# Moving a weight conversion between the slots of a fused top-k attention and GELU MLP

## The chip, the core and the metric

The kernel runs on one core of a Trainium2 chip. The core has a matrix engine (TensorE, PE in the profile), a vector engine (VectorE, DVE), a scalar engine (ScalarE, ACT), GpSimd (POOL) and an engine that here only issues DMAs (SyncE, SP). Each works through its own instruction queue in order and waits at semaphores for the others. The metric is the device time of one execution in microseconds; lower is better. Four runs of the kernel before took 1640.07 to 1641.21 us, median 1640.57.

## The reference

Attention with a top-k mask, then an MLP with an exact GELU:

```python
scores = scale * q @ k.T                        # (8, 8, 576, 576), head_dim 64
kth    = 32nd largest of each row of scores
scores = where(scores >= kth, scores, -1e9)
attn   = exp(scores - max); attn /= sum + 1e-9
x      = (attn @ v) -> (4608, 512)              # heads side by side
h      = x @ w_in                               # (512, 2048)
out    = gelu_exact(h) @ w_out                  # (2048, 512)
```

q, k and v are float32. Both weight matrices arrive as 64-bit floats, and the kernel makes float32 of them on the chip, with integer operations on their halves.

## The kernel before

**Items and slots.** Attention is cut into 144 items. An item is one block of 128 query rows for two heads (or the 64-row tails of two pairs), so two score rows of 576 per partition. The main loop runs over slots n = 0 to 147. Slot n holds the steps of four items at once, a pipeline by hand: scores of item n+2 (PE, copied out by ACT), the top-k of item n (DVE: eight MAX8 and six MATCH_REPLACE8, then the reciprocal `rden` of item n-1), the softmax of item n-1 (ACT: for each of its two rows e a Prelu that drops what is below the threshold, and an Exp that also sums into `den`), the transposes of item n-2 (PE into PSUM, copied to `pt` by ACT: the tails, then main 0, main 1), and the product with v of item n-3 (PE tile `o`, in even slots only, since two items share one; a copy to `xT` by ACT follows).

**What links the engines.** POOL makes the threshold of item n when its top-k is done (`neg`, `bias`, L355 and L358), adds the small constant to `den` (L372) when ACT has both sums, and multiplies the exponentials with `rden` (`normalise`, L392, two instructions); the transposes need these products. In some slots `normalise` runs on DVE instead. DVE's `rden` waits for POOL's L372, which waits for ACT's second softmax. The order on every engine is the order of the calls in the loop; nothing reorders them.

**PSUM.** The tag `tp` has two buffers, handed out in turn to the score tails `t_ps`, the product `o`, the transposes and the q/k transposes (`tp_qk`). So `o` holds one buffer until ACT has copied it to `xT`, and the second transposes after it (main 0) need that buffer.

**The MLP.** The loop calls `mlp` between the steps, which issues matmul pieces as soon as all heads of a block of tokens have their `xT`. The first block is complete in slot START = 10. In slots 10 and 11 at most four pieces are issued, later eight. What is left when the attention is done is issued behind the loop.

**The weights.** They are converted in 16 units of two blocks of 128 x 512. `ORDER` lists the units, `SLOT_OF` gives each its slot. For the unit of slot n: two DMAs of 512 KB bring its 64-bit words (`load_weights`, issued by SP at the end of slot n-2), ACT makes integer parts of them at the end of slot n-1 (`weights_size`, L175, L177 and, if POOL does not do it, L179), and in slot n POOL adds two parts (`weights_add`, L194) and the third (`weights_end`, L206). Where `on_pool` holds, POOL also does the multiplication (L191) in ACT's stead and `normalise` of that moment runs on DVE; where `ends_late` holds, the second addition stands in the middle of the slot, behind L372. The words lie in the upper half of `w_out_sb`, in one of two regions by the parity of the unit's place in `ORDER`; three units have a tile `words` of their own, because the region is by then in use. A region is loaded again when `weights_end` of its last unit is done.

Below are the functions that the diff touches and what calls them, with the line numbers of the profile.

## Time and profile before

| | us |
|---|---|
| median of four runs (lowest, highest) | 1640.57 (1640.07, 1641.21) |
| the profiled execution: time, span | 1640.07, 1638.3 |
| PE, DVE, ACT, POOL busy | 1586.6, 1415.0, 1185.2, 662.3 |
| a unit on ACT: L175, L177, L179, each | 1.24, 1.24, 1.13 |
| a unit on POOL: L194, L206, each; L191 where it runs | 2.40, 2.40; 3.12 |
| `normalise` of one item: POOL, DVE | 3.4, 0.95 |
| softmax of one row: L379, L380 and its accumulator read | 0.78, 0.78, 0.19 |
| DVE from slot to slot, slots 1 to 10 | 9.70 |

The span is what lies between the first and the last instruction; the time is 1.8 us longer. The first MAX8 of a slot marks where the slot begins on DVE: 10.68 us for slot 0, 20.34, 30.04, 39.74, 49.44, 59.15, 68.85, 78.55, 88.25, 97.95 for slots 1 to 9, 107.66 for slot 10, and 117.36, 129.13, 140.96, 151.73, 163.60, 173.32, 186.19, 195.91 and 206.35 for slots 11 to 19. The other engines begin their part of a slot earlier or later; ACT's parts of slots 4 to 9 begin some 3.5 us after DVE's. In the rows of a timeline the columns are the start, the time from the first start to the last end of the merged instructions, engine, line, operation, tiles, count, and in square brackets the idle time of the engine just before, with what ended it.

### The profile page before, as it was taken

To read this page: it belongs to the slowest core of one execution; us is meant where nothing else is said; L and a number is where in the kernel's file an instruction comes from. 1 tells how busy PE (TensorE), PEld (TensorE's weight loads), DVE (VectorE), ACT (ScalarE), POOL (GpSimd) and SP (SyncE) were. 2 spreads that over 40 slices of the span, in tenths; PEclk is the share of its full clock that TensorE was granted. 3 is DMA by queue.
4 is the path that set the end of the run, shared out by engine and by line. 5 is a ranking of instruction groups with operands and counts; after the bars stand their busy time and mean duration, and the time that the engine had idled before them with its cause. 6 is when DMAs were issued, how large, how long until landed. Compare 5 with 4: busy or idle time off the path is not lost.

```text
span 1638.3 us, 25030 instructions
## 1 busy us (share of the span) xinstructions
PE 1586.6 (97%) x8818; PEld 1075.4 (66%) x8818; DVE 1415.0 (86%) x3046; ACT 1185.2 (72%) x2133; POOL 662.3 (40%) x759
## 2 busy tenths in 40 slices
PE   6579999999999999999999999999999999999999
PEld 4356676766666666676666667676666666666665
DVE  7999999988898899998989898998889889999800
ACT  6999877777777777777777777777777777777720
POOL 4897533333333333333333333333333333333300
PEclk7779999999999999999999999999999999999999
DMA  6433110011101120001110111001110101000000
GB/s 166 142 110 121 55 43 1 14 33 40 35 1 28 30 50 8 14 16 36 30 28 15 28 30 43 1 14 32 41 36 1 28 16 35 1 14 3 5 13 13
DMA packets 126765, 56.14 MB, mean 34 GB/s; under 512 B 117776, under 2 KB 118064, under 8 KB 126640
## 3 DMA queue, kind: packets, MB, share of 16 engines
q1 hardware_dynamic: 125376, 54.12, 12.3%
q8 instruction: 70, 1.15, 0.3%
q10 hardware_dynamic: 1200, 0.39, 0.1%
q14 instruction: 55, 0.45, 0.1%
q0 software_dynamic: 64, 0.03, 0.0%
HBM read 45.08 MB, written 9.44 MB: 33 GB/s over the span
## 4 chain that ended last, share of the span: by engine, by line
PE 92%; ACT 5%; POOL 1%; issue 1%; DVE 1%; DMA 1%; SPq 0%; ACTq 0%; POOLq 0%; DVEq 0%
PE y_ps L554 30%; PE h_ps L518 30%; PE o L466 9%; PE tp L429 8%; PE s_ps L287 8%; PE tp_qk L242 2%; PE t_ps L283 2%; PE o L477 1%; ACT s L380 1%; PE s_ps L314 1%; PE tp_t L411 1%; ACT s L379 1%; POOL s L392 1%; ACT w_in_sb L175 1%; ACT s L297 1%
## 5 line engine op out<-in xcount | busy, mean ns | idle before, releaser
L340 DVE MAX8 top<-rest 128x8 f32<-128x576 f32 x864 | 608.8, 745 | 0.0
L518 PE MATMUL h_ps<-xT,w_in_sb 128*128 128x256 f32 (+1 forms) x2560 | 553.1, 361 | 0.0
L554 PE MATMUL y_ps<-w_out_sb,g 128*128 128x512 f32 x1152 | 548.9, 599 | 0.0
L392 POOL TENSOR_SCALAR s<-s,rden 128x576 f32<-128x576 f32 x278 | 476.5, 1723 | 0.6 <-DVE rden L366 0.4
L518 PEld LDWEIGHTS h_ps<-xT,w_in_sb 128*128 128x128 f32 x2560 | 428.4, 191 | 61.8 <-issue 16.8
L343 DVE MATCH_REPLACE8 rest<-top,rest 128x576 f32<-128x576 f32 x576 | 422.9, 741 | 0.0
L372 POOL TENSOR_SCALAR den<-den 128x2 f32<-128x2 f32 x144 | 32.0, 222 | 836.7 <-ACT s L380 836.3
L554 PEld LDWEIGHTS y_ps<-w_out_sb,g 128*128 128x128 f32 x1152 | 195.2, 190 | 168.2 <-issue 167.3
L297 ACT ACTIVATE s<-s_ps 128x1024 f32<-128x1024 f32 x127 | 130.4, 1027 | 164.7 <-PE s_ps L287 143.0
L380 ACT ACTIVATE s<-s,bias 128x576 f32<-128x576 f32 x288 | 223.3, 775 | 13.2 <-ACT s L379 0.8
L379 ACT ACTIVATE s<-s,neg 128x576 f32<-128x576 f32 x288 | 224.1, 778 | 0.3 <-POOL neg L355 0.2
L436 ACT COPY pt<-tp 128x512 f32<-128x512 f32 x256 | 147.1, 575 | 101.8 <-PE tp L429 101.8
L429 PEld LDWEIGHTS tp<-ident,s 128*128 128x128 f32 x1152 | 145.6, 144 | 100.5 <-issue 58.9
L343 DVE MATCH_REPLACE8 rest<-top,s 128x576 f32<-128x576 f32 x288 | 211.5, 742 | 0.0
L340 DVE MAX8 top<-s 128x8 f32<-128x576 f32 x288 | 201.6, 741 | 1.4 <-ACT s L293 1.4
L429 PE MATMUL tp<-ident,s 128*128 128x128 f32 x1152 | 177.8, 278 | 13.9 <-ACT pt L412 11.5
L466 PE MATMUL o<-pt,raw_v 128*64 128x256 f32 x1280 | 156.3, 392 | 0.0
L287 PE MATMUL s_ps<-qk 64*128 64x256 f32 x1024 | 150.9, 415 | 0.8 <-ACT s L295 0.8
L366 DVE RECIPROCAL rden<-den 128x2 f32<-128x2 f32 x144 | 23.0, 159 | 137.6 <-POOL den L372 137.3
L466 PEld LDWEIGHTS o<-pt,raw_v 128*64 128x64 f32 x1280 | 88.2, 140 | 66.6 <-issue 24.0
L287 PEld LDWEIGHTS s_ps<-qk 64*128 64x128 f32 x1024 | 91.1, 192 | 23.4 <-issue 1.3
L529 ACT ACTIVATE g<-h_ps 128x512 f32<-128x512 f32 x144 | 78.6, 595 | 37.8 <-PE h_ps L518 37.1
(71 smaller groups left out, 1073.9 us busy)
## 6 DMA issues: line engine op xcount, KB each, us to landing
raw_q<-in_q_dram SPq DMA_DIRECT2D x64, 128.0 KB, 2.4
raw_v<-in_v_dram SPq DMA_DIRECT2D x64, 128.0 KB, 2.4
w_out_sb<-in_moe_w_in_dram SPq DMA_DIRECT2D x16, 511.8 KB, 4.9
raw_k<-in_k_dram SPq DMA_DIRECT2D x62, 128.0 KB, 2.4
out_dram<-y SPq DMA_DIRECT2D x31, 256.0 KB, 2.2
w_out_sb<-in_moe_w_out_dram SPq DMA_DIRECT2D x10, 511.8 KB, 3.8
words<-in_moe_w_out_dram SPq DMA_DIRECT2D x6, 511.8 KB, 4.5
out_dram<-y SPq DMA_DIRECT2D x9, 128.0 KB, 2.3
```

The lines of the kernel that those rows point to most:

```text
L287: nc.tensor.matmul(s_ps[:, e, c * 256 : (c + 1) * 256], lhsT=lhsT[rows, :], rhs=qk[rows, KT + c * 256 : KT + (c + 1) * 256], start=True, s ...
L297: nc.scalar.activation(spread(s, S + TL, SM), s_ps, func=AF.Copy, scale=scale)
L340: nc.vector.max(st["top"][:, e, 8 * r : 8 * r + 8], cur[e])
L343: nc.vector.match_replace(rest[:, e], st["top"][:, e, 8 * r : 8 * r + 8], cur[e], LOWEST)
L379: nc.scalar.activation(s, s, func=AF.Prelu, bias=st["neg"][:, e, 1:2], scale=1.0, alpha=STEEP)
L380: nc.scalar.activation(s, s, func=AF.Exp, bias=st["bias"][:, e : e + 1], scale=1.0, accum_out=st["den"][:, e : e + 1],)
L392: (nc.vector if e >= 2 - on_dve else nc.gpsimd).tensor_scalar(s, s, st["rden"][:, e : e + 1], None, op0=ALU.mult)
L429: nc.tensor.transpose(tp[:, j * P : (j + 1) * P], s[:, first + j * P : first + (j + 1) * P], ident)
L436: nc.scalar.copy(out=dst, in_=tp.rearrange("p (j n) -> p j n", j=NM))
L466: nc.tensor.matmul(o[e * D : (e + 1) * D, 0:n], lhsT=vt[:, j, e, :], rhs=pt[:, e * NM + j if j < NM else 2 * NM, :], start=(j == 0), stop= ...
L518: nc.tensor.matmul(h_tile(u)[:, i, :], lhsT=w_in_sb[:, ko, f * P : (f + 1) * P], rhs=xT[:, ko, c0 : c0 + n], start=(ko == 0), stop=(ko == ...
L554: nc.tensor.matmul(y_of[sub], lhsT=g_of[u][:, i, sub * P : (sub + 1) * P], rhs=w_out_sb[:, f, :], start=(f == 0), stop=(f == FT - 1),)
```

## The change

The units move. Before, unit i of the order had slot i + 1, the last one slot 17. After, units 0 to 9 have slots 0 to 9, and the last six have slots 11, 13, 14, 15, 16 and 18; slots 10, 12 and 17 have none. With the slots move the DMAs, ACT's operations one slot earlier and POOL's. The third unit's words go to a tile of their own. All of the last six now have their multiplication on POOL (five before), and `normalise` runs on DVE at the end of slots 10, 12, 13, 14, 15 and 17 (before: 11, 12, 13, 14 and 16). The second addition of the first unit stands in slot 1, beside that of the second.

Up to slot 9 both rows of the softmax now stand ahead of the copy to `xT`; before, the copy stood between them. Slot 10 keeps the order it had.

```diff
-    FIRST = 1
     START = 2 * NP + 2
...
-    SLOT_OF = {u: FIRST + i + (i == UNITS - 1) for i, u in enumerate(ORDER)}
+    SLOT_OF = dict(zip(ORDER, [*range(START), 11, 13, 14, 15, 16, 18]))
...
-        if i not in (12, 14, 15):
+        if i not in (2, 12, 14, 15):
             at = FT // 2 + 4 * (i % 2)
...
     def on_pool(u):
-        return u in words and SLOT_OF[u] >= START + 2
+        return u in words and SLOT_OF[u] > START
...
     def ends_late(u):
-        return u in words and SLOT_OF[u] <= START
+        return u in words and SLOT_OF[u] < START
...
     for n in range(2):
-        load_weights(FIRST + n)
+        load_weights(n)
...
+    weights_size(unit_in(0))
...
         if n <= START:
             softmax(n - 1, 0)
+        if n < START:
+            softmax(n - 1, 1)
         copy_x()
         mlp(1)
...
-        if not late:
+        if n == START:
             softmax(n - 1, 1)
...
-        if ends_late(unit_in(n)):
-            weights_end(unit_in(n))
+        for u in (unit_in(0), unit_in(1)) if n == 1 else (unit_in(n),) if n > 1 else ():
+            if ends_late(u):
+                weights_end(u)
...
-        if n >= FIRST:
-            load_weights(n + 2)
+        load_weights(n + 2)
```

## The prediction

> **What bounds the kernel now.** I read the page's slices first, then busy time slot by slot, then the chain of waits up to 250 us, then POOL's and PE's timelines. The slices:

> ```profile
> PE   6579999999999999999999999999999999999999
> DVE  7999999988898899998989898998889889999800
> PEclk7779999999999999999999999999999999999999
> ```

> A slice is 41 us. PE is full from the fourth on; nothing behind it touches a weight conversion. What can move is where PE's full stretch begins, and its gaps. The slots 9 to 12 (columns: length, then busy time and count of PE, PE weight loads, DVE, ACT, POOL; granted clock, DMA share, GB/s):

> ```profile
> 97.95:107.66 9.71, 4.17 (x21) 2.80 (x20) 9.71 (x24) 8.83 (x16) 8.86 (x8) 0.74 0.30 108
> 107.66:117.36 9.70, 9.56 (x50) 6.50 (x51) 9.70 (x24) 9.28 (x17) 8.20 (x8) 0.73 0.32 111
> 117.36:129.13 11.77, 9.75 (x60) 7.62 (x58) 10.74 (x25) 10.88 (x18) 11.27 (x11) 1.00 0.63 189
> 129.13:140.96 11.83, 11.06 (x67) 8.63 (x65) 10.77 (x24) 11.66 (x20) 8.87 (x7) 1.00 0.27 97
> ```

> Up to slot 10 DVE has no gap, and ACT and POOL are within a microsecond of it. From slot 10 on PE is full but for the difference of the first two figures: 0.14, 2.02 and 0.77 us. What starts slot 10's MLP stands in the chain (start, length, what):

> ```profile
> 96.37 0.67 PE tp L429 x4
> 97.06 0.52 ACT pt L436
> ...
> 98.04 1.26 ACT w_out_sb L175
> ...
> 106.01 1.13 PE tp L429 x4
> 107.17 0.59 ACT pt L436
> 107.80 0.80 PE t_ps L283 x2
> 108.60 2.01 PE s_ps L287 x8
> 110.61 3.46 PE o L466 x20
> 114.33 0.87 PE h_ps L518 x4
> ```

> From 64.8 to 107.8 us the chain is ACT and the transposes it waits for; then PE runs slot 10's scores and `o`, and the first MLP matmul follows. So ACT's pace through slots 1 to 9 sets where the long stretch begins, and DVE is close beside it. PE's later gaps:

> ```profile
> 125.24 0.66 PE L429 MATMUL tp<-ident,s 128*128 128x128 f32 x4 [0.64 <-ACT pt L412]
> 127.77 0.49 PE L283 MATMUL t_ps<-qk 128*128 128x128 f32 x2 [1.39 <-ACT pt L436]
> 137.47 0.66 PE L429 MATMUL tp<-ident,s 128*128 128x128 f32 x4 [0.77 <-ACT pt L412]
> 199.97 0.30 PE L416 MATMUL tp_t<-ident,s 128*64 128x128 f32 x1 [0.71 <-POOL s L392]
> ```

> They are 3.5 us together: the most that relief behind slot 10 can give. It is also 0.2% of the time, about what a measurement of this kernel can tell from no change.

> **The change part by part**, followed along ACT.

> *First unit, slot 0.* A unit's three ACT operations take 3.47 us (19.89 to the next scores copy at 23.36). They now follow the q/k copy at 14.78, in ACT's own idle time (1.65 and 1.20 us before rows there): 15.3 to 18.75, if the words have landed (issued from 7.79, landing after 3.6 to 6.8 us: yes). Scores copy (1.06) and q/k copy (0.48) follow, so unit 1 starts at 20.3, 0.4 us behind where unit 0 started. ACT is one unit further and 0.4 us late. SP issues the third unit's two DMAs (1.0 us) at 21.5 instead of 30.5 into a tile of its own; v's four issues behind them, 1 us later, are read only at 52.5.

> *POOL in slot 1: the first cost.* Before:

> ```profile
> 28.11 2.41 POOL L206 TENSOR_TENSOR w_in_sb<-w_in_sb,w_out_sb 128x1024 int32<-128x1024 int32 x1
> 30.48 0.23 POOL L355 TENSOR_SCALAR neg<-top 128x4 f32<-128x4 f32 x1
> 30.79 0.19 POOL L358 TENSOR_TENSOR bias<-neg 128x2 f32<-128x2 f32 x1
> 30.97 3.44 POOL L392 TENSOR_SCALAR s<-s,rden 128x576 f32<-128x576 f32 x2
> ```

> Now two additions stand behind L372: 28.4 to 33.2 (2 x 2.37). Queued behind them are `neg` and `bias` (33.7) and `normalise` (37.1 against 34.4). ACT's softmax of item 1 waits for `neg` (33.5 against 32.83) and ends at 36.8; the tails' transposes wait for `normalise`: 37.2 against 34.46. In slot 2 the q/k transposes and the tails' were ready before ACT came for them (36.05); now ACT waits for both, and the next unit starts at 41.2 instead of 39.14. ACT is 2.0 us late. POOL's L372 of slot 2, behind L194 (37.1 to 39.6), makes `rden` 0.2 us late on DVE.

> *Copy behind both softmaxes, slots 4, 6, 8.* In slot 4 ACT saves its 0.30 us wait for `o`. But main 0 needs the buffer that this copy frees. Before, PE made main 0 during the second softmax. Now ACT waits: copy 0.35, transposes 0.66, minus the tails' copy in between. From the copy's start to the next unit was 3.31 us in slot 6, with 1.58 of softmax in it: 1.73. Now: 1.10 to main 0's copy, then two copies, 2.08. Cost 0.35 each in slots 6 and 8, 0.05 in slot 4. Queued behind on ACT: main 1, the next unit, scores, softmax; behind those L372 and `rden`. The price rests on PE's full clock. The nearest rows on both sides: main 0 at 75.59 after 1.32 us of idle PE took 0.65; main 1 at 47.11 after 1.96 us took 1.12, with the granted clock at 0.50 in that slot. PE's gap ahead of main 0 grows from 1.3 to 2.9 us. At half clock both transposes cost 1.30 a slot instead of 0.35. I take 0.35, because a gap of 4.49 us (60.3 to 64.80) still started at full clock (0.33 for one transpose); the upper end stays in the range.

> [...] The trace shows drops after 3.55 and 3.66 us and none at the start after 4.49. [...]

> *To slot 9.* ACT's units before started at 39.14, 49.60, 59.44, 69.05, 78.50, 88.09, 98.04, 107.91. From 41.2 with the same steps and these costs: 51.7, 61.55, 71.15, 80.95, 90.55, 100.85, and slot 9's last copy 2.8 us later than before. ACT does not catch up: its steps are 9.5 to 10.4, DVE's 9.70. DVE now waits for L372 in slots 2, 4, 5 and 9, 1.3 us together, inside ACT's 2.8. Loads still land in time: they go out later with POOL, but are used later too.

> *Slots 9 to 12: the gain.* The unit that ACT did at 107.91 is gone, but the MLP's start waits for PE's `o`, not for ACT: nothing. So it starts at 114.2 + 2.8. At slot 10's end ACT does 2.45 us for the next unit instead of 3.47; the tails of slot 11 come 1.0 earlier, which removes the gap of 0.64; main 0 then waits for PE, and main 1's copy still stands behind the second softmax, so 0.47 of 2.02 us is gained. At slot 11's end no unit (2.45): the gap of 0.77 goes. DVE's `normalise` at slot 10's end (0.95) replaces slot 11's; POOL does slot 11's in 3.4 us, 3 us before PE needs it. POOL's 7.9 us of unit 10 end at 126 + 2.8, before L372's sums.

> *Slots 15 to 18.* The unit of slot 16 adds 2.45 us on ACT at 175.6, where ACT had 0.51 and 0.93 us idle: the tails' copy goes from 180.46 to 182.3, and main 0, which needs its buffer, 0.6 us late on PE. POOL's `normalise` at slot 16's end (3.4 us, DVE's 0.95 before) ends at 189.3 against PE's tails at 189.99: covered by 0.7, else the excess counts in full. At slot 17's end DVE's `normalise` removes the 0.71 us gap at 199.97. Slot 18's unit falls on 1.1 us of idle ACT, and its PE matmuls do not wait for it.

> Sum: +2.8 - 0.5 - 0.8 + 0.6 - 0.7 = +1.4. The profiled execution of 1640.07 (span 1638.3 and 1.8 around it) gives 1641.5; it stood 0.5 below the median, so against the median 1642.0.

> **The rivals.**
> A. *Clock stays up, ACT's delay is hidden.* PE's gaps in slots 5, 7 and 9 shorten, because ACT comes 2 to 3 us later and `normalise` only 1.6 to 2.5. If the clock holds there, each main 1 takes 0.66 instead of 1.12 (1.4 together), and slot 10's `t_ps`, `s_ps` and `o` take 0.49, 1.13 and 2.38 instead of 0.80, 2.08 and 3.53 (2.4 together). Then 1.4 - 3.8 = -2.4: 1638.2. [...]
> B. *Half clock in slots 4, 6 and 8.* Main 0 and main 1 of the product slots at 1.1: 3 x 0.95 more, +4.3: 1644.9. It decides (3.3 us) from two of the three slots on. For: main 1 at 47.11. Against: the 4.49 gap.
> C. *The move is hidden.* POOL's second addition is absorbed because ACT's wait in slot 2 only replaces waits for the half-clock transposes there (0.72 and 0.27 us idle) and the rest is regained behind slot 10: -0.5 to +0.5, about 1640.6. Against: ACT has no idle time in slots 3 to 9 to catch up.

> **How the numbers follow.** Forecast 0.42 (1640.9 to 1643.4 by itself), A 0.24, B 0.22, C 0.12. Faster by over 0.2% (below 1637.3): less than half of A, whose middle lies 0.9 above that bound, 0.10. Slower (above 1643.8): nearly all of B and 0.05 of the forecast, 0.25. The rest 0.65. The range reaches down into A to 1637.7, with 0.1 of it left out below, and up to 1645.8, which is B and 0.9 us of waits in slots 16 to 18.

> **What would show it.** Right: `neg` of slot 1 near 33.3 us and `normalise` near 33.7; a unit on ACT at about 41; ACT idle some 0.7 us ahead of main 0 in slots 4, 6 and 8; the first MLP matmul near 117; no wait at L412 in slots 11 and 12, a wait of some 1.5 us for main 1's copy at the end of slot 11. Wrong: the first MLP matmul at or before 114; words that land late in slot 0 or 2; the granted clock in slots 4 to 10 far from 0.7 to 0.8; waits of PE behind slot 13 that before did not have.

## The result and the profile after

The changed kernel took 1644.41 us (median of 35 runs, 1642.62 to 1647.14), the kernel before 1640.97 (55 runs, 1639.53 to 1643.60). The ratio is 1.0021 with a 95% interval of 1.0016 to 1.0026: 3.4 us slower (2.6 to 4.3), against a forecast of 1.4. The profiled execution took 1643.92 us with a span of 1642.1, 3.8 more than before. In it DVE starts slot 0 0.2 us later, because k's first load landed later (PE waited 0.21 us for it).

The page's slices after:

```profile
PE   5569999999999999999999999999999999999999
DVE  7999989988898989998989888998889888999800
PEclk7769999999999999999999999999999999999999
```

The picture is the same: PE and its clock differ in the first three slices of 41 us alone, where PE is a little emptier; behind them only some of DVE's digits differ, by one. Slots 9 to 12, with the columns as before:

```profile
99.80:111.25 11.45, 5.95 (x28) 4.33 (x28) 9.81 (x23) 9.70 (x16) 8.74 (x8) 0.65 0.27 92
111.25:122.01 10.76, 10.51 (x58) 7.28 (x58) 10.65 (x24) 6.82 (x15) 7.17 (x9) 0.77 0.01 2
122.01:131.73 9.72, 8.09 (x49) 6.51 (x48) 9.72 (x23) 8.49 (x15) 7.91 (x4) 1.00 0.57 160
131.73:143.35 11.62, 11.62 (x72) 9.19 (x73) 10.75 (x25) 10.72 (x19) 4.97 (x8) 1.00 0.25 99
```

Slot 9 is now 11.45 us long, with DVE busy for 9.81 of it; before, DVE never waited there. Slot 11 still has PE idle for 1.6 us, slot 12 has no gap any more. The chain of waits ahead of the first MLP matmul:

```profile
99.62 1.97 PE tp L429 x8
...
102.56 3.43 POOL s L392 x2
105.99 2.38 POOL w_out_sb L194
...
109.95 0.87 ACT s L380 x2
111.03 1.13 PE tp L429 x4
112.18 0.59 ACT pt L436
112.81 0.80 PE t_ps L283 x2
113.61 2.01 PE s_ps L287 x8
115.62 2.61 PE o L466 x20
118.49 0.87 PE h_ps L518 x4
```

From the softmax of slot 9 on it is the same chain, 4 to 5 us later: the transposes for main 1 start at 111.03 (106.01 before), the chain's first MLP piece at 118.49 (114.33). Just ahead of that softmax it runs through POOL's `normalise` and an addition, where before it ran through ACT's unit. PE's gaps behind it, from its timeline:

```profile
131.61 0.49 PE L283 MATMUL t_ps<-qk 128*128 128x128 f32 x2 [1.39 <-ACT pt L436]
185.41 0.66 PE L429 MATMUL tp<-ident,s 128*128 128x128 f32 x4 [0.48 <-ACT pt L412]
203.75 0.41 PE L416 MATMUL tp_t<-ident,s 128*64 128x128 f32 x2 [1.17 <-ACT s L298]
```

The waits of 0.64 and 0.77 us at L412 in slots 11 and 12 are gone and the one for main 1's copy is unchanged. Slots 16 and 18 have new ones, 0.48 and 1.17; the 0.71 on POOL is gone. At the start of ACT's work for one unit, or of one of PE's slots, the trace after lies behind the trace before by:

| place | before | after | later by |
|---|---|---|---|
| DVE's first MAX8 | 10.68 | 10.90 | 0.2 |
| ACT's unit at the end of slot 2 | 39.14 | 41.30 | 2.2 |
| slot 3 | 49.60 | 52.15 | 2.6 |
| slot 4 | 59.44 | 62.45 | 3.0 |
| slot 5 | 69.05 | 72.08 | 3.0 |
| slot 6 | 78.50 | 81.86 | 3.4 |
| slot 7 | 88.09 | 91.51 | 3.4 |
| slot 8 | 98.04 | 103.05 | 5.0 |
| PE's first MLP matmul, slot 10 | 114.17 | 118.33 | 4.2 |
| PE's score tails, slot 12 | 127.77 | 131.61 | 3.8 |
| slot 13 | 140.78 | 143.63 | 2.9 |
| slot 17 | 185.91 | 189.46 | 3.6 |
| slot 19 | 207.89 | 211.78 | 3.9 |

After slot 19 nothing changes up to the end of the span.

### The profile page after: what moved, and what is told of

Its sections match the earlier page's. It is cut to its first block, busy times and chain, and to the rows that moved or that the text cites. A ratio compares the mean times of both kernels' runs of the same rounds, so it can differ in the third digit from the quotient of the medians.

```text
span 1642.1 us, 25024 instructions
## 1 busy us (share of the span) xinstructions
PE 1588.5 (97%) x8818; PEld 1076.9 (66%) x8818; DVE 1416.4 (86%) x3048; ACT 1185.2 (72%) x2132; POOL 662.1 (40%) x758
## 4 chain that ended last, share of the span: by engine, by line
PE 92%; ACT 5%; POOL 1%; issue 1%; DMA 1%; SPq 0%; DVE 0%; ACTq 0%; POOLq 0%; DVEq 0%
PE h_ps L518 31%; PE y_ps L554 30%; PE o L466 8%; PE tp L429 8%; PE s_ps L287 8%; PE tp_qk L242 2%; PE t_ps L283 2%; PE o L477 1%; PE tp_t L411 1%; ACT s L380 1%; PE s_ps L314 1%; ACT s L379 1%; POOL s L392 1%; ACT s L297 0%; ACT w_out_sb L179 0%
## 5 line engine op out<-in xcount | busy, mean ns | idle before, releaser
L518 PE MATMUL h_ps<-xT,w_in_sb 128*128 128x256 f32 (+1 forms) x2560 | 553.0, 361 | 0.0
L392 POOL TENSOR_SCALAR s<-s,rden 128x576 f32<-128x576 f32 x276 | 473.0, 1723 | 0.8 <-issue 0.4
L518 PEld LDWEIGHTS h_ps<-xT,w_in_sb 128*128 128x128 f32 x2560 | 428.4, 191 | 61.8 <-issue 16.4
L372 POOL TENSOR_SCALAR den<-den 128x2 f32<-128x2 f32 x144 | 32.0, 222 | 842.1 <-ACT s L380 842.0
L436 ACT COPY pt<-tp 128x512 f32<-128x512 f32 x256 | 146.9, 575 | 104.8 <-PE tp L429 104.8
L429 PEld LDWEIGHTS tp<-ident,s 128*128 128x128 f32 x1152 | 146.4, 144 | 102.5 <-issue 58.2
L429 PE MATMUL tp<-ident,s 128*128 128x128 f32 x1152 | 178.1, 279 | 16.3 <-ACT pt L412 8.7
L466 PE MATMUL o<-pt,raw_v 128*64 128x256 f32 x1280 | 155.9, 391 | 0.0
L287 PE MATMUL s_ps<-qk 64*128 64x256 f32 x1024 | 151.8, 417 | 0.8 <-ACT s L295 0.8
L466 PEld LDWEIGHTS o<-pt,raw_v 128*64 128x64 f32 x1280 | 87.9, 139 | 66.5 <-issue 24.1
L287 PEld LDWEIGHTS s_ps<-qk 64*128 64x128 f32 x1024 | 91.6, 193 | 23.4 <-issue 1.1
L529 ACT ACTIVATE g<-h_ps 128x512 f32<-128x512 f32 x144 | 78.6, 595 | 37.8 <-PE h_ps L518 37.1
```

What stands on the lines that cost most here:

```text
L287: nc.tensor.matmul(s_ps[:, e, c * 256 : (c + 1) * 256], lhsT=lhsT[rows, :], rhs=qk[rows, KT + c * 256 : KT + (c + 1) * 256], start=True, s ...
L392: (nc.vector if e >= 2 - on_dve else nc.gpsimd).tensor_scalar(s, s, st["rden"][:, e : e + 1], None, op0=ALU.mult)
L429: nc.tensor.transpose(tp[:, j * P : (j + 1) * P], s[:, first + j * P : first + (j + 1) * P], ident)
L436: nc.scalar.copy(out=dst, in_=tp.rearrange("p (j n) -> p j n", j=NM))
L466: nc.tensor.matmul(o[e * D : (e + 1) * D, 0:n], lhsT=vt[:, j, e, :], rhs=pt[:, e * NM + j if j < NM else 2 * NM, :], start=(j == 0), stop= ...
L518: nc.tensor.matmul(h_tile(u)[:, i, :], lhsT=w_in_sb[:, ko, f * P : (f + 1) * P], rhs=xT[:, ko, c0 : c0 + n], start=(ko == 0), stop=(ko == ...
```

## The experiments

Three theories stood for the 3.4 us: P, the first ten units cost it through POOL's two additions in slot 1; C, the place of the copy to `xT` costs it; L, the last units do, by waits in slots 16 and 18. Differences below are the ratio to the kernel before on the same chip, times 1640.8 us, with its interval.

### One part at a time: the copy

```diff
         if n <= START:
             softmax(n - 1, 0)
+        if n < START:
+            softmax(n - 1, 1)
         copy_x()
...
-        if not late:
+        if n == START:
             softmax(n - 1, 1)
```

> The kernel before with only the copy to xT moved behind both softmaxes up to slot 9. Theory P (POOL): the loss of the change, 3.4 us, comes mostly from the first ten units, through POOL's two additions in slot 1; then this costs what ACT waits ahead of main 0, 0.05 + 0.35 + 0.35 = 0.8 us, 1.7 if one of the three slots runs its transposes at half clock. Rival C (copy): the copy's place is the whole loss; then this costs 3 us or more. Rival L (last units): the loss comes from the waits in slots 16 and 18; then this costs nothing.

Measured: ratio 1.0010 (1.0001 to 1.0019), 1.6 us slower (0.2 to 3.1). L's zero is just out; C as the whole loss is at the edge (3.1 against 3 or more), and the next run, slower by 2.6 with the copy in its old place, rules it out. PE's timeline of this run, slots 4, 6 and 8:

```profile
58.36 1.09 PE L429 MATMUL tp<-ident,s 128*128 128x128 f32 x8 [2.29 <-ACT xT L471]
...
77.74 1.97 PE L429 MATMUL tp<-ident,s 128*128 128x128 f32 x8 [2.28 <-ACT xT L471]
...
97.98 1.85 PE L429 MATMUL tp<-ident,s 128*128 128x128 f32 x8 [2.94 <-ACT xT L471]
```

Main 0 and main 1 now wait for the copy and run in one go. In slot 4 the eight transposes take 1.09 us; in slots 6 and 8 they run at about half speed, 1.97 and 1.85. So two of three slots paid the upper price that the prediction had named.

### The first ten units

```diff
-    FIRST = 1
...
-    SLOT_OF = {u: FIRST + i + (i == UNITS - 1) for i, u in enumerate(ORDER)}
+    SLOT_OF = dict(zip(ORDER, [*range(START), 11, 12, 13, 14, 15, 17]))
...
-        if i not in (12, 14, 15):
+        if i not in (2, 12, 14, 15):
...
-        load_weights(FIRST + n)
+        load_weights(n)
...
+    weights_size(unit_in(0))
...
-        if ends_late(unit_in(n)):
-            weights_end(unit_in(n))
+        for u in (unit_in(0), unit_in(1)) if n == 1 else (unit_in(n),) if n > 1 else ():
+            if ends_late(u):
+                weights_end(u)
...
-        if n >= FIRST:
-            load_weights(n + 2)
+        load_weights(n + 2)
```

> The kernel before with only the first ten units one slot earlier; the last six stay in slots 11 to 15 and 17, the copy stays between the softmaxes. Theory P: +2.0 from POOL in slot 1 and some 0.4 from words that land late in slot 4, nothing given back behind slot 10: 2.0 to 2.8 us slower. ACT's units in slots 3 to 9 come 2 us later than before. Rivals C and L: within 0.5 us of the kernel before.

Measured: 1.0016 (1.0007 to 1.0024), 2.6 us slower (1.1 to 3.9). The total is P's number. ACT's units of slots 3 to 8 begin at 52.35, 62.93, 72.55, 82.00, 91.62 and 102.35: 2.8 to 4.3 us later than before, where 2 were expected. The profiled execution is 1.3 us above the median of this kernel.

### The last six units

```diff
-    SLOT_OF = {u: FIRST + i + (i == UNITS - 1) for i, u in enumerate(ORDER)}
+    SLOT_OF = dict(zip(ORDER, [*range(1, 11), 11, 13, 14, 15, 16, 18]))
...
-        return u in words and SLOT_OF[u] >= START + 2
+        return u in words and SLOT_OF[u] > START
```

> The kernel before with only the last six units in slots 11, 13 to 16 and 18, all on POOL. Theory P: -0.5 in slot 11 and -0.8 in slot 12 for shorter waits on ACT, +0.6 in slot 16, +0.5 in slot 18: within 0.5 us of the kernel before. Rival L: 1.5 us slower or more. If the relief counted in full, 2 us faster.

Measured: 0.9997 (0.9989 to 1.0006), between 1.8 faster and 1.0 slower. L as the loss is out. PE's timeline has the two new waits here too, 0.49 in slot 16 and, in slot 18:

```profile
201.55 0.41 PE L416 MATMUL tp_t<-ident,s 128*64 128x128 f32 x2 [1.18 <-ACT s L298]
```

The three parts sum to 1.6 + 2.6 - 0.5 = 3.7 us, against 3.4 for the whole; each of the three has an interval of about 1.4 us either way.

### The second addition of the first unit back in slot 0

```diff
-        for u in (unit_in(0), unit_in(1)) if n == 1 else (unit_in(n),) if n > 1 else ():
+        for u in (unit_in(n),):
             if ends_late(u):
                 weights_end(u)
```

> The changed kernel with the second addition of the first unit in slot 0, where POOL is idle, instead of slot 1. Theory P: neg and normalise of slot 1 come at about 31 us, ACT's unit at 41.3 comes at about 39.4, and 2.0 of the 3.4 us are gone: about 1.4 us slower than the kernel before. Rivals C and L: still 3 us slower or more.

Measured: 1.0013 (1.0005 to 1.0022), 2.1 us slower (0.8 to 3.6); 1.3 less than the changed kernel, where 2.0 were expected. The intervals overlap, so the time alone does not exclude the rivals' 3 us; the trace has to tell. POOL made `neg` at 31.16 and `normalise` at 31.63, as expected. But ACT's unit came at 40.40, not 39.4: the words of the third unit, whose load was issued at 21.90, were late:

```profile
29.64 1.24 ACT L175 ACTIVATE w_in_sb<-words,low 128x1024 int32<-128x1024 int16 x1 [0.50 <-DMA words<-in_moe_w_in_dram]
```

In the run with the first ten units alone the same wait was 0.70 us; in the profiled execution of the changed kernel it was not there.

### The last unit behind slot 18's scores copies

In the changed kernel:

```diff
-        weights_add(unit_in(n))
+        if n != 18:
+            weights_add(unit_in(n))
         scores(n + 2)
+        if n == 18:
+            weights_size(unit_in(n))
+            weights_add(unit_in(n))
...
-        weights_size(unit_in(n + 1))
+        if n != 17:
+            weights_size(unit_in(n + 1))
```

> The changed kernel with the last unit's ACT operations, and POOL's, behind the scores copies of slot 18 instead of ahead of them. Theory W: the last unit turned the hoped-for gain of slot 18 into a wait of 1.17 us for the buffer that L298 frees; with the copy first this wait goes: 1.2 us less than the changed kernel, some 2.2 us slower than the kernel before. Rival: the wait only moves to the copy to xT, which now comes behind the unit: no difference to the changed kernel (3.4 us).

Measured: 1.0016 (1.0007 to 1.0025), 2.6 us slower. The times alone do not tell the two readings apart, 0.8 less than the changed kernel being inside the intervals; the trace does. ACT's timeline of slot 18:

```profile
199.99 1.02 ACT L297 ACTIVATE s<-s_ps 128x1024 f32<-128x1024 f32 x1 [0.20 <-PE s_ps L287]
200.91 0.27 ACT L298 ACTIVATE s<-t_ps 128x128 f32<-128x128 f32 x1
201.06 1.26 ACT L175 ACTIVATE w_out_sb<-words,low 128x1024 int32<-128x1024 int16 x1
```

L298 ran at 200.91 instead of 203.45, and the wait of 1.17 us ahead of the tails' transposes is gone. But part of it moved to the copy to `xT` at 203.49, as the rival had it: PE's weight load for the seventh MLP matmul waits for that copy, and these eight matmuls take 2.23 us instead of 1.89.

```profile
203.89 0.30 PEld L518 LDWEIGHTS h_ps<-xT,w_in_sb 128*128 128x128 f32 x2 [0.47 <-ACT xT L471]
```

PE's score tails start 0.4 us earlier than in the changed kernel in slot 18 (198.43 against 198.82) and 1.3 us earlier in slot 19 (210.49 against 211.78), so slot 18 gained 0.9 of the 1.2 us.

### Keeping PE's clock up

Nine extra matmuls behind the scores of slots 3, 5, 7 and 9, in the changed kernel and in the kernel before:

```diff
         tr = transposes(n - 2)
+        if 2 < n and n < START and n % 2:
+            for _ in range(9):
+                nc.tensor.matmul(warm[:, 0:P], lhsT=idle, rhs=idle, start=True, stop=True)
```

> The changed kernel with nine extra matmuls 128x128 on PE behind the scores in slots 3, 5, 7 and 9, results unused. Theory K (clock): in slots 3 to 10 PE's transposes, scores and o run at half clock because of its idle time; ACT waits 0.72 us for them in every odd slot and the start of the MLP waits for 5 us of half-clock scores and o. With the gaps filled the transposes take 0.66 instead of 1.11 us, the wait at main 1 in odd slots falls to about 0.3, slot 10's scores and o take 1.5 and 2.4 instead of 2.9 and 2.9: 2 to 4 us faster than the changed kernel, so -0.5 to +1.4 against the kernel before. Rival: the clock does not matter because DVE and POOL hold the pace: no gain, +3.4.

> The kernel before with the same extra matmuls. Theory K: 0.45 us in each of slots 5, 7 and 9 and 2.4 in slot 10: 2.5 to 4 us faster than the kernel before. Rival (DVE holds the pace): within 0.7 us of it.

Measured: 1.0015 (1.0006 to 1.0024) for the changed kernel, 2.5 us slower; 0.9995 (0.9986 to 1.0003) for the kernel before. Both gained some 0.8 us, less than theory K asked for and inside the intervals. The clock rose in part only. In the changed kernel main 1 took 0.66 us in slot 7 and still 1.11 in slots 3, 5 and 9, though PE waited about equally long for ACT ahead of it in all four (2.45 to 2.69 us). In the kernel before it took 0.66 to 0.69 in slots 3, 5 and 7 but 1.12 in slot 9, and in slots 4 and 6, where it had taken 0.66, it now took 1.11. Slot 10's score tails still took 0.80 us in both, half clock.

### A version that beats both

The kernel before with the last six units moved, the last one behind slot 18's scores copies, and the nine extra matmuls (the three diffs above together); without these matmuls; and with six more of them ahead of main 1:

> The kernel before with the last six units in slots 11, 13 to 16 and 18, the last one's ACT and POOL work behind slot 18's scores copies, and the extra matmuls; the first ten units and the copy to xT as before. From the single parts: -0.5 for the six, -1.2 for slot 18, -2.5 to -4 for the clock if theory K holds: 4 to 5.7 us faster than the kernel before. If K falls: 1.7 us faster.

> The combined kernel without the extra matmuls: the kernel before with the last six units moved and the last one's work behind slot 18's scores copies. From the parts: -0.5 - 1.2 = 1.7 us faster than the kernel before; the combined one was 1.9 faster, so if this equals it, the extra matmuls bring nothing there.

> The combined kernel with six more extra matmuls ahead of main 1 in slots 3, 5, 7 and 9, where PE still waits 1.6 to 2.5 us for ACT. If the granted clock is what keeps slot 10's scores and o at half speed: these take 1.5 and 2.4 us instead of 2.9 and 3.5, another 1.5 to 2 us, 3.5 to 4 us faster than the kernel before. If the clock drops there for another reason: as the combined one, 1.9 faster.

Measured: 0.9988 (0.9979 to 0.9996), 0.9995 (0.9986 to 1.0004) and 0.9990 (0.9981 to 0.9999). The combined kernel is 2.0 us faster than the kernel before (0.7 to 3.4) and about 5 faster than the changed one. That the extra matmuls bring something there, 1.2 us by the medians' ratios, is not clear of the intervals. The six more brought nothing that shows. The profiled execution of that kernel is the slowest of its eleven (1641.08 against a median of 1639.11), so its timeline shows what happened in it, not what held the others. PE in slot 10:

```profile
108.96 1.14 PE L287 MATMUL s_ps<-qk 64*128 64x256 f32 x8
110.02 2.38 PE L466 MATMUL o<-pt,raw_v 128*64 128x256 f32 x20
113.75 0.33 PE L411 MATMUL tp_t<-ident,s 128*128 128x128 f32 x1 [1.35 <-POOL s L392]
113.92 1.03 PE L518 MATMUL h_ps<-xT,w_in_sb 128*128 128x256 f32 x4
```

The scores and `o` did run at full clock (1.14 and 2.38, against 2.08 and 3.53 in the kernel before), but now the tails' transposes, which stand ahead of the MLP in PE's queue, waited 1.35 us for POOL's `normalise`. POOL was late because ACT was: its L372 came at 107.09 behind ACT's sums, against 105.51 with fewer extra matmuls. The first MLP matmul came at 113.92, against 113.77. In slot 12 of this execution the scores took 2.08 us again, against 1.13 in slot 11.

### The change with its three costs taken back

The changed kernel with the addition in slot 0, slot 18's order, and the copy between the softmaxes:

> The changed kernel with the three costs taken back: first unit's second addition in slot 0, the copy to xT between the softmaxes again, the last unit behind slot 18's scores copies. What stays is the first ten units one slot earlier and the last six spread. If the costs found are the whole story: 3.4 - 1.4 (addition) - 1.6 (copy) - 1.2 (slot 18) = -0.8, so 0.3 to 1.5 us faster than the kernel before. If the earlier slots cost by themselves (words that land late in slots 1 and 4, 0.4 to 0.7 us each): 0 to 1 us slower. Still 3 us slower: none of the three was the cause.

Measured: 0.9998 (0.9989 to 1.0007), between 1.8 faster and 1.1 slower. All of the loss is gone, so the three together are its cause; how it splits among them rests on the traces, since the intervals of the single parts overlap. ACT's units of slots 2 and 3 began at 39.56 and 50.33 (39.14 and 49.60 before; 41.30 and 52.15 in the changed kernel). By themselves the earlier slots bring nothing that shows: the combined kernel without the extra matmuls, which has units 0 to 9 in their old slots, stands at 0.9995. Whether they cost a little is inside the interval; the words of slot 4 are still late here, by 0.49 us.

## Why the prediction was right and where it fell short

The direction was right, and so was the mechanism of the largest cost, POOL in slot 1. The forecast of 1.4 us was too small by 2.0, inside the stated range. The result also lies near the 3.3 us of rival B with two slots at half clock, but by chance: in the profiled execution one slot paid that price, and the rest came from elsewhere. One of the signs of being wrong appeared: a wait of PE behind slot 13 that was not there before and not forecast, at 203.75.

- **POOL in slot 1, 2.0 us on ACT.** Right. POOL's timeline after:

```profile
28.68 4.77 POOL L206 TENSOR_TENSOR w_in_sb<-w_in_sb,w_out_sb 128x1024 int32<-128x1024 int32 x2
33.42 0.23 POOL L355 TENSOR_SCALAR neg<-top 128x4 f32<-128x4 f32 x1
33.73 0.19 POOL L358 TENSOR_TENSOR bias<-neg 128x2 f32<-128x2 f32 x1
33.90 3.44 POOL L392 TENSOR_SCALAR s<-s,rden 128x576 f32<-128x576 f32 x2
```

  `normalise` was forecast for 33.7 and began at 33.90; ACT's next unit was forecast for 41.2 and began at 41.30, 1.9 us late when the later start is taken off.

- **"Loads still land in time."** Wrong by 0.44 us in slot 4, where ACT's row shows the wait:

```profile
62.45 1.23 ACT L175 ACTIVATE w_out_sb<-w_out_sb,low 128x1024 int32<-128x1024 int16 x1 [0.44 <-DMA w_out_sb<-in_moe_w_out_dram]
```

  The load was issued at 56.27, behind eight issues of q and k that themselves waited for a PE step of slot 3 now 2.5 us later, and the chain of waits runs through those issues. Another 0.43 us went between a Prelu and its Exp in slot 3. All five experiments with the earlier slots show this gap as well (0.40 to 0.43), none of the others does; its cause is open.

- **The copy, 0.35 us in slots 6 and 8 and 0.05 in slot 4.** Right in slots 4 and 6 (0.0 without the late load, and 0.3), wrong in slot 8: 1.6. The step that failed is the choice of full clock from one gap that seemed to leave it up. The row behind that gap, before the change, already spoke against it: the first transpose ran at full clock, the four behind it took 0.89 us, between the 0.66 of full and the 1.06 to 1.12 of half clock, and main 1 at 67.42 took 1.11.

```profile
64.80 0.33 PE L411 MATMUL tp_t<-ident,s 128*128 128x128 f32 x1 [4.49 <-POOL s L392]
64.96 0.89 PE L429 MATMUL tp<-ident,s 128*128 128x128 f32 x4
```

  So the clock did fall after the gap of 4.49 us, a moment into the burst: the trace has it at 1.00 up to 65.13 us and at 0.50 from there. PE's timeline after the change:

```profile
80.21 1.09 PE L429 MATMUL tp<-ident,s 128*128 128x128 f32 x8 [2.90 <-ACT xT L471]
...
99.62 1.97 PE L429 MATMUL tp<-ident,s 128*128 128x128 f32 x8 [2.48 <-ACT xT L471]
```

  Rival B's mechanism took place, in one slot of three here and in two of three with the copy alone.

- **The MLP starts as late as ACT's last copy.** Nearly: `o` of slot 10 took 2.68 us instead of 3.53, which gave 0.85 back. That is a piece of rival A.

- **Slots 9 to 12, 1.3 us regained.** Right in total: the lag falls from 4.2 at the first MLP matmul to 2.9 at slot 13, 0.3 of it by slot 12 and 1.0 in it (0.5 and 0.8 forecast). The gap of 1.39 stayed, as said.

- **Slot 16, +0.6.** Right: 0.7 from slot 13 to slot 17, by the wait at 185.41 that was named, on the tails' copy.

- **Slot 18, -0.7.** This step failed with the wrong sign: 0.3 lost instead. The sentence that "its PE matmuls do not wait for it" counts ACT's idle time and the matmuls that read the unit, and leaves out the other buffer: `tp` has two, `t_ps` of the scores holds one until L298 has copied it, and L298 now stood behind 2.45 us of conversion. With the order turned around this wait was gone, though 0.3 us of it came back at the copy to `xT`.

In sum: slot 18 +1.0 against the forecast, the clock in slot 8 +1.2, the late words +0.4, the Exp +0.4, the faster `o` -0.9, smaller differences within 0.2; with the later start of 0.2 that is the 3.8 us between the two spans to within 0.1. Rival C, that the move is hidden, is out: from slot 3 to slot 9 ACT's idle times are waits for transposes that follow its own copies (0.27 to 1.04 us), the late words and the open 0.43 us, and none of these can make up a lag.

## What to carry to other kernels

When work moves on an engine that, as ACT here, takes it in the order of the calls, write down what it now stands ahead of and which buffers those instructions free; idle time on that engine is not cover if a copy that another engine waits for stands behind the work (PE's 1.17 us in slot 18). A lag on a second engine that is as full as the first was not worked off: 2 us lost in slot 1 were still there eight slots later. A step that became free of one bound (the clock in slot 10) gained only up to the next one: in the one execution that shows it, the tails' transposes then waited 1.35 us for POOL, which was late behind ACT.

## What the runs showed of the hardware

```profile
75.24:78.65 3.41, 2.02 (x17) 1.00 0.67 256
78.65:82.07 3.42, 1.62 (x12) 1.00 0.00 0
95.72:99.14 3.42, 1.42 (x13) 1.00 0.19 77
99.14:102.55 3.41, 2.93 (x13) 0.50 0.00 0
...
61.72:65.13 3.41, 0.33 (x3) 1.00 0.94 322
65.13:68.55 3.42, 1.85 (x10) 0.50 0.32 72
```

The changed kernel's bursts at 80.21 and 99.62 lie in the second row of their pair. Ahead of the first PE had been busy for 2.02 us and the clock stayed at 1.00; ahead of the second for 1.42, and it was 0.50. In the kernel before PE was busy for 0.33 us up to 65.13, and the clock fell there, in the middle of a burst. Between 20 and 125 us the two traces have 22 such stretches at 1.00. All nine in which PE was busy for 0.00 to 1.62 us were followed by 0.50, all 13 with 1.99 to 3.42 us by 1.00. The ten stretches of 0.50 after which the clock came back had PE busy for 2.93 us or more; after two of 3.17 and 3.25 us in the kernel before it stayed at 0.50. So the length of the gap just ahead of a burst did not tell its clock, and PE's busy time in the stretch before did in these two traces. Whether it also tells where the extra matmuls kept the clock up was not shown.
